# Four-chunk FP32 sums of query-key products by GpSimd additions and accumulating DMAs, gate products ahead of softmax, and four gate buffers

## The chip, the cores and the metric

The kernel runs on one NeuronCore of a Trainium2 chip. The metric is the device time of one execution in microseconds (us), and lower is better. Times vary by some 0.3% between executions, so every comparison below is between kernels run in turn on the same chip. The granted TensorE clock was 1.0.

The profile names engines briefly: PE is TensorE's matrix multiplication, PEld its weight loads, DVE is VectorE, ACT is ScalarE, POOL is GpSimd, SP the queue that issues most DMAs. "L839" is a line of the kernel's source; the line numbers of the two kernels differ.

## The reference, cut to what matters

```python
xn = layernorm(x)                                  # x: 2048 x 640, bf16
# A: sliding, dilated attention, 32 heads of 20, window of 8 keys, 2 apart
q, k, v = split(xn @ wqkv)
logits = einsum("bhsd,bhswd->bhsw", q, k_window) * 20 ** -0.5
o = einsum("bhsw,bhswd->bhsd", softmax(logits), v_window)
# B: bilinear gated feed-forward, 1536 wide
h = (xn @ w_gate) * (xn @ w_up)
return x + o @ wo + h @ w_down
```

The sequence is worked in four blocks of 512 positions. The 640 channels of q and k lie in five chunks of 128 partitions. A logit is a sum over 20 channels that lie in four partitions of each of the five chunks: VectorE multiplies q by shifted k, and TensorE, with a 128x32 matrix of ones and zeros, adds up partitions and chunks.

## The kernel before

A small scheduler in the kernel orders the tasks of five in-order engines by an own model of durations and by priorities (a lower number goes first). It fixes the order when the program is built; on the chip an engine that waits holds everything behind it. The three parts that the change touches follow.

The last block's products are summed over pairs of chunks in FP32 before they reach TensorE:

```python
def pair_add(j, s, n, q0, f, parts):          # f: the two FP32 product tiles, 128 x 1024
    a, b = PRD32[f[0]], PRD32[f[1]]
    o = s[:, q0:q0 + 2, :]                    # bf16
    def go():
        op("pool", lambda e: e.tensor_tensor(o, a[:], b[:], ALU.add), r=[a[:], b[:]], w=[o], ..., occ=2.36, lock=True)
        free.extend(f)
    yield Task("pool", go, r=[a[:], b[:]], w=[o], prio=5, lock=True)
# ... two pair tiles for each of two half-windows, and chunk 4 alone: six tiles, 24 matmuls for the block's logits
```

Gate and up products. Each half of h is five matmuls into a PSUM bank; ScalarE copies the gate half to SBUF, VectorE multiplies it by the up half and so frees that bank:

```python
yield Task("act", ev, r=[PS[:, hold[0], :]], w=[h], prio=7)
yield Task("dve", mul, r=[h, PS[:, hold[1], :]], prio=15)      # softmax tasks on VectorE: prio 10
```

The attention-weighted values: VectorE multiplies (`PV`), GpSimd adds two halves (`SV<-PV`), TensorE sums partitions.

```python
def ht(j, m):                                  # buffers of h: three sets for four blocks
    return HX[m][:] if j % 3 == 2 else HT[:, j % 3, m, :]
```

Of the kernel before, what the change touches and what calls it, by code (L numbers as in the profile page):

```python
# [6 lines left out]
ALU = mybir.AluOpType  # L7

S = 2048
D = 640  # L10
NCH = 5
# [37 lines left out]
class Sched:  # L49
# [5 lines left out]
    def __init__(self, nc):  # L55
        self.nc = nc
        self.ops = []
        self.state = {}
        self.base = {}
        self.clock = {e: nc.alloc_semaphore(f"clk_{e}") for e in ("act", "pe", "dve", "pool")}  # L60
        self.n_dma = 0
        self.t = {"sp": 0.8, "act": 0.8, "pe": 1.26, "dve": 0.9, "pool": 0.8}
        self.t_lock = 0.0
        self.t_data = 0.0
        self.pe_mode = 0
        self.threads = []
        self.banks = {b: 0.0 for b in range(8)}
        self.seq = 0
        self.groups = {}
        self.n_eng = {e: 0 for e in ENGINES}  # L70
# [55 lines left out]
    def op(self, eng, fn, r=(), w=(), dma=False, name="", occ=None, lat=None, lock=False, nbytes=0, mode=0, group=None, extra=0.0):  # L126
# [17 lines left out]
        if dma:  # L144
            self.t[eng] = start + (0.48 if occ is None else occ)
            self.t_data = max(self.t_data, start + 1.2) + nbytes / 280e3
            X.end = self.t_data + 0.8 + extra
        else:
            self.t[eng] = start + occ
            X.end = start + (occ if lat is None else lat)  # L150
# [190 lines left out]
def build_kernel(nc, A_x, A_wqkv, A_wo, B_x, B_w_gate, B_w_up, B_w_down, out):  # L341
# [62 lines left out]
    WIDE = (3,)  # L404
# [6 lines left out]
    STATS = sb("STATS", [128, NT, 16], FP32)  # L411
    MV = sb("MV", [128, NT, 16], FP32)
    SD = sb("SD", [128, NT, 16], FP32)
# [10 lines left out]
    def ht(j, m):  # L424
        return HX[m][:] if j % 3 == 2 else HT[:, j % 3, m, :]

    WPOS = (2, 0, 1)
# [234 lines left out]
    def proj_qk():  # L662
# [11 lines left out]
        for j in (2, 3):  # L674
            yield have("xnt", 4 * j + 3)
            for m in range(NCH):
                for which in (0, 1):
                    if which or j not in WIDE or m == NCH - 1:
# [33 lines left out]
    def slot():  # L712
        return free.pop(0)
# [7 lines left out]
    def products():  # L721
        for j in range(NJ):
            slots = []
            if j in WIDE:
                yield from wide(j, slots)
            for r in (1, 0):
                for c in range(NCH - 1 if j in WIDE else 0, NCH):
                    yield num(4, "qk", 0, j, c)
                    yield num(4, "qk", 1, j, c)
                    yield lambda: len(free) > 0  # L730
                    n = slot()
                    s = PRD[n]
                    kv, rk = k_view(j, r, c, 0, 4)
                    q = QT[:, j, c, :]
                    qb = q.unsqueeze(1).to_broadcast([128, 4, JB])

                    def go(s=s, qb=qb, kv=kv, q=q, rk=rk):
                        op("dve", lambda e: e.tensor_tensor(s[:], qb, kv, ALU.mult), r=[q, rk], w=[s[:]],  # L738
                           name=f"prod{j}_{r}_{c}", occ=1.15, lock=True)

                    yield Task("dve", go, r=[q, rk], w=[s[:]], prio=20 + j, lock=True)
                    slots.append((n, s, r))
            K.spawn(logits(j, slots))

    def q_bank(j, c, hold):
        def go(b):
            mms([(PS[:, b, :], 0, c, j * JB, JB)], b, f"p0_{j * JB}")
            hold.append(b)
            for _ in range(4):
                bump("qk", 0, j, c)  # L750

        yield have("xnt", 4 * j + 3)
        yield Task("pe", go, r=[wcols(0, NCH - 1, c), XNT[:, NCH - 1, j * JB:(j + 1) * JB]], prio=8, banks=1, keep=1)

    def wide(j, slots):
        for c0 in (0, 2):
            hold = {}
            for c in (c0, c0 + 1):
                hold[c] = []
                yield num(4, "qk", 1, j, c)  # L760
                K.spawn(q_bank(j, c, hold[c]))
            last = None
            for r in (1, 0):
                yield lambda: len(free) > 0
                n = slot()
                s = PRD[n]
                parts = []
                for q0 in (0, 2):
                    f = []
                    for c in (c0, c0 + 1):  # L770
                        yield lambda: len(hold[c]) > 0 and len(free) > 0
                        k = slot()
                        f.append(k)
                        o = PRD32[k]
                        kv, rk = k_view(j, r, c, q0, 2)
                        q = PS[:, hold[c][0], :]
                        qb = q.unsqueeze(1).to_broadcast([128, 2, JB])

                        def go(o=o, qb=qb, kv=kv, q=q, rk=rk):
                            X = op("dve", lambda e: e.tensor_tensor(o[:], qb, kv, ALU.mult), r=[q, rk], w=[o[:]],  # L780
                                   name=f"prow{j}_{r}_{c}_{q0}", occ=1.17)
                            if r == 0 and q0 == 2:
                                K.free_bank(hold[c][0], X)

                        yield Task("dve", go, r=[q, rk], w=[o[:]], prio=20 + j)
                    K.spawn(pair_add(j, s, n, q0, f, parts))
                slots.append((n, s, r, parts))

    def pair_add(j, s, n, q0, f, parts):
        a, b = PRD32[f[0]], PRD32[f[1]]  # L790
        o = s[:, q0:q0 + 2, :]

        def go():
            op("pool", lambda e: e.tensor_tensor(o, a[:], b[:], ALU.add), r=[a[:], b[:]], w=[o], name=f"padd{j}_{n}_{q0}",  # L794
               occ=2.36, lock=True)
            free.extend(f)
            parts.append(q0)

        yield Task("pool", go, r=[a[:], b[:]], w=[o], prio=5, lock=True)

    def logits(j, slots):
# [5 lines left out]
        nt = len(slots) // 2  # L807

        def go(*bs):
            for i, e in enumerate(slots):  # L810
                n, s, r = e[:3]
                b, i = bs[1 - r], i % nt
# [30 lines left out]
    def softmax(x):  # L843
# [24 lines left out]
        def attn():  # L868
            op("dve", lambda e: e.tensor_tensor(L[:], L[:], bc(RS[:], 8), ALU.mult), r=[L[:], R], w=[L[:]], name="attn",
# [61 lines left out]
    def unit(u):  # L931
# [33 lines left out]
        def add(x):  # L965
            o, p = SV[u % NS][:, 2 * x:2 * x + 2, :], slots[x]
            X = op("pool", lambda e: e.tensor_tensor(o, p[:, :, 0, :], p[:, :, 1, :], ALU.add), r=[p[:]], w=[o],  # L967
# [8 lines left out]
        def adder(x, slots=slots, u=u, add=add):  # L976
            yield Task("pool", lambda: add(x), r=[slots[x][:]], w=[SV[u % NS][:, 2 * x:2 * x + 2, :]], prio=10, lock=True)
# [16 lines left out]
        if len(pend) == 3 or u == NU - 1:  # L994
# [29 lines left out]

    def gu(j):
# [10 lines left out]
        elif j == 2:  # L1036
            yield have("atx", 1)
        else:
            yield num(8, "dn", j - 3)
        if j:  # L1040
            yield have("gu", j - 1)
        for m in range(NF):
            h = ht(j, m)
            if j == 1 and m == 6:
                yield num(NJ, "lg")
            hold = []
# [9 lines left out]
            def after(h=h, hold=hold, j=j, m=m):  # L1056
# [11 lines left out]
                yield Task("dve", mul, r=[h, PS[:, hold[1], :]], prio=15)  # L1068
# [18 lines left out]
    def dn(j):  # L1087
        yield num(NF, "h", j)
        yield num(NCH, "ot", j)
        if j:  # L1090
            yield num(8, "dn", j - 1)
        for st in range(4):
            t = 4 * j + st
            pieces = ((0, 320), (320, 480), (480, 640)) if t == NT - 1 else ((0, 320), (320, 640))
            for nb, (c0, c1) in enumerate(pieces):
                rows = slice(st * TS, (st + 1) * TS)
                cols = slice(c0, c1)
                wid = c1 - c0
                hold = []
                yield have("xr", t)  # L1100

                def go(b):
                    n = NF + NCH
                    dst = PS[:, b, 0:wid]
                    for i in range(n):
                        if i < NF:
                            l, x = ht(j, i)[:, rows], WD[:, i, cols]
                        else:
                            l, x = OT[:, j, i - NF, rows], WO[:, i - NF, cols]
                        op("pe", (lambda l, x, i: lambda e: e.matmul(dst, l, x, start=(i == 0),  # L1110
                                                                    stop=(i == n - 1)))(l, x, i),
                           r=[l, x], w=[PS[:, b, :]], name=f"dn{t}_{nb}_{i}", occ=wid / 2400 + 0.0025, lat=0.25)
                    hold.append(b)
                    bump("dn", j)

                def fin_thread(t=t, nb=nb, cols=cols, hold=hold, wid=wid):
                    o, xr = FOUT[:, t % 2, cols], XR[:, t % NXR, cols]

                    def fin():
                        b = hold[0]  # L1120
                        X = op("dve", lambda e: e.tensor_tensor(o, PS[:, b, 0:wid], xr, ALU.add), r=[PS[:, b, :], xr], w=[o],  # L1121
                               name=f"fin{t}_{nb}", occ=0.15 + wid / 960)
                        K.free_bank(b, X)

                    def store():
                        if t == NT - 1:
                            f, d = o, ohbm[t * TS:(t + 1) * TS, cols]
                        else:
                            f, d = FOUT[:, t % 2, :], ohbm[t * TS:(t + 1) * TS, :]
# [97 lines left out]
```

## Time and profile before

| | before |
|---|---|
| time, median (3 runs) | 271.63 us (271.47 to 271.93) |
| profiled span | 269.7 us |
| TensorE busy | 264.3 us, 98% |
| VectorE busy | 231.9 us, 86% |
| GpSimd busy | 115.2 us, 43% |

The page of the profile gives busy time of each engine, its share of the span and the number of instructions; its part 4 gives the shares of the chain of work that ended last.

```profile
PE 264.3 (98%) x1791; PEld 152.7 (57%) x1791; DVE 231.9 (86%) x294; ACT 98.4 (36%) x175; POOL 115.2 (43%) x65
...
PE 96%; DVE 2%; DMA 1%; issue 0%; DVEq 0%
```

TensorE bounds the kernel: nearly the whole chain is its own work. A gain has to come from TensorE's work or from its waits. The chain in order of time (start us, length us, what) has one place after the start-up where it leaves TensorE:

```profile
108.68 13.05 PE PS L1052 x60
121.73 0.08 issue
...
122.62 0.69 DVE HT L1061
...
123.36 18.52 PE PS L1052 x85
```

Timeline: start us, us, engine, line, operation, number of instructions, and in brackets the idle time before them.

```profile
121.57 1.24 PE L1052 MATMUL PS<-XNT,WG 128*128 128x512 bf16 x5
123.36 1.25 PE L1052 MATMUL PS<-XNT,WU 128*128 128x512 bf16 x5 [0.55 <-DVE HT L1061]
```

The five matmuls from 121.57 us take 5 x 0.216 = 1.08 us, so the next could have started at 122.65 us and started at 123.36 us: 0.71 us late, of which the profile shows 0.55 us as idle after the last matmul's end. The second group waited for a bank that a gate product on VectorE frees. VectorE's timeline at that time:

```profile
115.22 1.22 DVE L845 TENSOR_TENSOR SM<-LOG 128x1024 f32<-128x1024 bf16 x1
116.47 3.19 DVE L845 TENSOR_TENSOR SM<-SM 128x512 f32<-128x512 f32 x2
...
121.48 1.22 DVE L869 TENSOR_TENSOR LOG<-LOG,RS 128x2048 bf16<-128x2048 bf16 x1
122.62 2.47 DVE L1061 TENSOR_TENSOR HT<-HT,PS 128x512 bf16<-128x512 bf16 x4
```

GpSimd's timeline at that time:

```profile
115.38 3.27 POOL L967 TENSOR_TENSOR SV<-PV 128x1024 bf16<-128x1024 f32 x1 [11.69 <-DVE PV L962]
```

The VectorE lines are the end of the second softmax (sums, reciprocal, scaling) and then four gate products. The two small sums at 116.47 us took 3.19 us together, against 1.15 us for the same two in the first softmax (at 68.05 us), and GpSimd's addition beside them took 3.27 us instead of 2.36.

### The profile page before, as it was taken

Reading aid. Unit: us, or ns where it says so; the run is one execution under the profiler, and the core shown is the slowest. Engines: PE = TensorE matmul, PEld = TensorE weight load, DVE = VectorE, ACT = ScalarE, POOL = GpSimd, SP = SyncE. Lnnn points to the kernel's source line nnn. Section 1 sums busy time; section 2 is a strip of 40 time slices with the busy share of each in tenths; the row PEclk is TensorE's granted clock in tenths of the full one; section 3 lists DMA queues with packets and bytes.
Section 4 is the critical chain, followed back from the end, with each engine's and each line's share of the span. In section 5 each row is a group of like instructions: output and inputs, shape, how many; then the busy total and the mean of one; then the engine's idle time right before and its main releaser. Section 6 shows DMA issues by size and latency. Waiting matters only on the chain.

```text
span 269.7 us, 4474 instructions
## 1 busy us (share of the span) xinstructions
PE 264.3 (98%) x1791; PEld 152.7 (57%) x1791; DVE 231.9 (86%) x294; ACT 98.4 (36%) x175; POOL 115.2 (43%) x65
## 2 busy tenths in 40 slices
PE   7999999999999999999999999999999999999995
PEld 4896965544444444443444446764447767654775
DVE  4778899999999997999999999989999998984221
ACT  2469998557632123632324422015240120033000
POOL 1000000000018763042776676957868679755000
DMA  7966479322325934901295333555333655220101
GB/s 209 366 198 86 99 124 381 158 97 97 104 44 163 216 66 130 282 5 30 52 256 125 86 79 79 155 153 130 79 80 106 175 135 148 66 81 2 49 27 50
DMA packets 39717, 33.49 MB, mean 124 GB/s; under 512 B 15376, under 2 KB 38416, under 8 KB 39696
## 3 DMA queue, kind: packets, MB, share of 16 engines
q1 hardware_dynamic: 39408, 33.15, 45.8%
q8 instruction: 14, 0.23, 0.4%
q10 hardware_dynamic: 288, 0.05, 0.1%
q14 instruction: 7, 0.06, 0.1%
HBM read 25.08 MB, written 5.26 MB: 112 GB/s over the span
## 4 chain that ended last, share of the span: by engine, by line
PE 96%; DVE 2%; DMA 1%; issue 0%; DVEq 0%
PE PS L1052 38%; PE PS L1110 28%; PE PS L610 24%; PE PS L816 3%; PE PS L1008 2%; DMA XST<-in_A_x_dram 1%; PE PS L569 1%; DVE STATS L525 0%; DVE XNT L578 0%; DVE HT L1061 0%; DVE XNS L543 0%; DVE FOUT L1121 0%; DVE MV L528 0%; DVE SD L536 0%; DVEq L319 0%
## 5 line engine op out<-in xcount | busy, mean ns | idle before, releaser
L967 POOL TENSOR_TENSOR SV<-PV 128x1024 bf16<-128x1024 f32 x40 | 94.7, 2378 | 48.4 <-DVE PV L962 48.3
L962 DVE TENSOR_TENSOR PV<-VX,PS 128x1024 f32<-128x1024 bf16 (+1 forms) x56 | 92.7, 1670 | 0.0
L610 PE MATMUL PS<-XNT,WQKV 128*128 128x512 bf16 (+2 forms) x480 | 67.0, 299 | 0.8 <-DVE XNT L578 0.8
L1052 PE MATMUL PS<-XNT,WU 128*128 128x512 bf16 x240 | 59.7, 379 | 0.5 <-DVE HT L1061 0.5
L1052 PE MATMUL PS<-XNT,WG 128*128 128x512 bf16 x240 | 59.7, 379 | 0.0
L610 PEld LDWEIGHTS PS<-XNT,WQKV 128*128 128x128 bf16 x480 | 43.4, 114 | 23.4 <-DVE XNT L578 1.5
L1110 PE MATMUL PS<-WD,HT 128*128 128x320 bf16 (+1 forms) x300 | 43.3, 294 | 0.0
L615 ACT ACTIVATE HT<-PS 128x512 bf16<-128x512 f32 x36 | 21.5, 597 | 53.2 <-PE PS L1052 53.1
L1052 PEld LDWEIGHTS PS<-XNT,WU 128*128 128x128 bf16 x240 | 23.3, 98 | 29.3 <-DVE HT L1061 1.0
L1052 PEld LDWEIGHTS PS<-XNT,WG 128*128 128x128 bf16 x240 | 23.2, 98 | 28.7 <-issue 0.8
L738 DVE TENSOR_TENSOR PRD<-QT,KT 128x2048 bf16<-128x2048 bf16 x32 | 36.8, 1218 | 0.0
L1110 PEld LDWEIGHTS PS<-WD,HT 128*128 128x128 bf16 x300 | 28.5, 98 | 11.6 <-issue 1.3
L794 POOL TENSOR_TENSOR PRD<-PRF,PRF 128x1024 bf16<-128x1024 f32 x8 | 18.8, 2357 | 35.5 <-DVE PRF L780 35.5
L1121 DVE TENSOR_TENSOR FOUT<-PS,XR 128x320 bf16<-128x320 f32 (+1 forms) x33 | 15.8, 478 | 18.3 <-PE PS L1110 18.2
L1061 DVE TENSOR_TENSOR HT<-HT,PS 128x512 bf16<-128x512 bf16 x36 | 24.1, 682 | 6.8 <-PE PS L1052 5.6
L1110 PE MATMUL PS<-WO,OT 128*128 128x320 bf16 (+1 forms) x165 | 27.1, 295 | 0.0
L835 POOL MEMSET LOG<- 32x6 bf16 (+6 forms) x7 | 0.4, 95 | 46.6 <-ACT LOG L827 46.6
L1017 ACT ACTIVATE OT<-PS 128x512 bf16<-128x512 f32 x20 | 10.5, 597 | 25.1 <-PE PS L1008 25.1
L1110 PEld LDWEIGHTS PS<-WO,OT 128*128 128x128 bf16 x165 | 15.9, 98 | 5.9
L780 DVE TENSOR_TENSOR PRF<-PS,KT 128x1024 f32<-128x1024 f32 x16 | 19.0, 1218 | 0.3 <-PE PS L816 0.2
L525 DVE BATCH_NORM_STATS2 STATS<-XST 128x6 f32<-128x320 bf16 x32 | 14.7, 469 | 2.0 <-DMA XST<-in_A_x_dram 2.0
L947 ACT ACTIVATE PS<-ATX 128x512 f32<-128x512 bf16 x8 | 4.8, 598 | 27.4 <-DVE PV L962 27.4
(47 smaller groups left out, 162.3 us busy)
## 6 DMA issues: line engine op xcount, KB each, us to landing
VX<-v_scratch SPq DMA_DIRECT2D x80, 130.0 KB, 2.9
XST<-in_A_x_dram SPq DMA_DIRECT2D x16, 160.0 KB, 6.3
v_scratch<-VST SPq DMA_DIRECT2D x4, 640.0 KB, 4.4
XR<-in_A_x_dram SPq DMA_DIRECT2D x16, 160.0 KB, 3.3
out_dram<-FOUT SPq DMA_DIRECT2D x15, 160.0 KB, 2.0
WG<-in_B_w_gate_dram SPq DMA_DIRECT2D x1, 1920.0 KB, 7.6
WU<-in_B_w_up_dram SPq DMA_DIRECT2D x1, 1920.0 KB, 11.8
WD<-in_B_w_down_dram SPq DMA_DIRECT2D x1, 1920.0 KB, 8.6
```

Of the source, the lines that this page charges most:

```text
L525: op("dve", lambda e: e.bn_stats(o, a), r=[a], w=[("st", t, i)], name=f"bn{t}_{i}", occ=0.49)
L610: op("pe", (lambda o, l, x, c, first: lambda e: e.matmul(o, l, x, start=first, stop=(c == NCH - 1)))(o, l, x, c, first), r=[l, x], w=[o], ...
L615: X = op("act", (lambda o, i: lambda e: e.activation(o, i, ACT.Copy))(o, i), r=[i], w=[o], name=name, occ=0.12 + n * 0.9e-3)
L738: op("dve", lambda e: e.tensor_tensor(s[:], qb, kv, ALU.mult), r=[q, rk], w=[s[:]], name=f"prod{j}_{r}_{c}", occ=1.15, lock=True)
L780: X = op("dve", lambda e: e.tensor_tensor(o[:], qb, kv, ALU.mult), r=[q, rk], w=[o[:]], name=f"prow{j}_{r}_{c}_{q0}", occ=1.17)
L794: op("pool", lambda e: e.tensor_tensor(o, a[:], b[:], ALU.add), r=[a[:], b[:]], w=[o], name=f"padd{j}_{n}_{q0}", occ=2.36, lock=True)
L962: op("dve", lambda e: e.tensor_tensor(p, vw, a, ALU.mult), r=[vv] + rk, w=[p], name=f"pv{u}_{x}_{r0}", occ=0.09 + 1.1 * nr)
L967: X = op("pool", lambda e: e.tensor_tensor(o, p[:, :, 0, :], p[:, :, 1, :], ALU.add), r=[p[:]], w=[o], name=f"pva{u}_{x}", occ=2.36, lock= ...
L1052: op("pe", (lambda l, x, c: lambda e: e.matmul(PS[:, b, :], l, x, start=(c == 0), stop=(c == NCH - 1)))(l, x, c), r=[l, x], w=[PS[:, b, :] ...
L1061: X = op("dve", lambda e: e.tensor_tensor(h, h, PS[:, hold[1], :], ALU.mult), r=[h, PS[:, hold[1], :]], w=[h], name=f"h{m}_{j}", occ=0.65)
L1110: op("pe", (lambda l, x, i: lambda e: e.matmul(dst, l, x, start=(i == 0), stop=(i == n - 1)))(l, x, i), r=[l, x], w=[PS[:, b, :]], name=f" ...
L1121: X = op("dve", lambda e: e.tensor_tensor(o, PS[:, b, 0:wid], xr, ALU.add), r=[PS[:, b, :], xr], w=[o], name=f"fin{t}_{nb}", occ=0.15 + wi ...
```

## The change

The intent: fewer logit matmuls in the last block (four tiles instead of six), by summing four chunks in FP32, partly on GpSimd and partly by DMAs that add into their destination; no gate product behind a softmax; and more freedom of order through a fourth set of h buffers and a down projection in two parts. The diff has some 300 lines; this is its core.

```diff
-    WIDE = (3,)
+    QUAD = {3: (1, 0)}
+    BY_DMA = (((0, 0), (0, 2)), ((1, 0), (1, 2)))
     ...
+    def sum32(j, r, q0, p, a, b):
+        x, y = PRD32[a][:], PRD32[b][:]
+        if (r, q0) in BY_DMA[p]:
+            yield Task("pool", lambda: op("pool", lambda e: e.dma_start(x, y, accum_op=ALU.add), r=[x, y], w=[x], dma=True,
+                                          name=name, occ=0.88, acc=3.3), r=[x, y], w=[x], prio=4)
+        else:
+            yield calm
+            yield Task("pool", lambda: op("pool", lambda e: e.tensor_tensor(x, x, y, ALU.add), r=[x, y] + tokens(), w=[x], ...
+        free.append(b)
     ...
+            if acc:                                    # the scheduler's model of such a DMA
+                self.t_acc = max(self.t_acc, start + 2.8) + acc
     ...
+    def calm():                                        # GpSimd additions stay out of a softmax
+        return all(("sm", x) in done or count.get(("logits", x), 0) < 2 for x in range(2))
     ...
     def ht(j, m):
-        return HX[m][:] if j % 3 == 2 else HT[:, j % 3, m, :]
+        if j == 3:                                     # block 3 uses the dead normalized input of blocks 0 to 2
+            return XNT[:, m % NCH, m // NCH * JB:(m // NCH + 1) * JB]
+        return HX[HXM[m]][:] if j == 2 else HT[:, j, m, :]
     ...
+                if on_pool(j, m):                      # some gate products on GpSimd, after the second softmax
+                    yield Task("act", uev, r=[PS[:, hold[1], :]], w=[us], prio=7)
+                    yield Task("pool", pmul, r=[h, us], w=[h], prio=HP_PRIO, lock=True)
+                    return
-                yield Task("dve", mul, r=[h, PS[:, hold[1], :]], prio=15)
+                yield Task("dve", mul, r=[h, PS[:, hold[1], :]], prio=H_PRIO)      # H_PRIO = 9
     ...
-                yield Task("pe", go, prio=40, banks=1, r=[WD[:], WO[:]])           # 12 down + 5 output matmuls
+        yield Task("pe", down, prio=41, banks=1, keep=..., r=[WD[:], WO[:]])       # 12, and in another task 5
```

GpSimd still makes eight additions of 128x1024 for the sums. The order of instructions shows the last block's logits on TensorE behind 30 gate/up groups of five matmuls, where there were 24 in front of them, and 11 of the 48 gate products on GpSimd.

## The prediction

> **What bounds it now.** TensorE. The page shows PE busy 264.3 of 269.7 us, and the chain of waits that ended last is 96% PE. Along that chain TensorE starts at 5.38 us, is busy without a break from about 16.8 us, waits once, and ends at 267.0 us. Its pieces run at one rate: 80 gate/up matmuls of 512 columns in 17.27 us (216 ns each), 136 down/output matmuls of 320 columns in 18.58 us (137 ns). The one wait, in the chain at 121.73 to 123.36 us, is 1.63 us: a gate/up matmul wants a PSUM bank that a VectorE gate product must free, and the timeline shows VectorE in the second softmax until 122.6 us, four gate products behind it. The granted clock is 1.00 throughout.
>
> **What the change does.**
> 1. Last block's logits: six product tiles become four, so 24 matmuls become 16. The 24 took 1.41 us, the 40 of another block 2.27; I expect 0.95, saving 0.46 us, all on the chain.
> 2. Gate products ahead of softmax on VectorE: the 1.63 us wait should go, all on the chain.
> 3. GpSimd still makes eight 128x1024 additions (2.36 us each), but now in a chain over four chunks, plus four accumulating DMAs of 0.52 MB. The Trainium skill ("DMA: Bandwidth & Descriptors", section on the anatomy of a GpSimd DMA) gives 2.0 us plus bytes over 436 GB/s: 3.2 us for a plain copy; reading the destination as well should make it 4 to 6. No trace here has one. Instruction order puts these logits 6 gate/up units later on TensorE (30 in front instead of 24): 107.3 becomes about 113.7 us. Adding up VectorE products (1.13 us apart), DMAs and additions, the last sum ends near 112 to 113 us: just in time; DMAs one microsecond slower each would cost 1 to 3 us.
> 4. That starts the second softmax about 6 us later. Before, VectorE was 97% busy from 125 to 163 us and 94% to 237; so 11 of the 48 gate products go to GpSimd (estimate 1.2 us each, half a 2.36 us addition; ScalarE copies their up half first, 0.6 us each), which takes 11 x 0.68 = 7.5 us off VectorE. GpSimd's busy sum rises from 115 to about 128 us, VectorE's falls to about 224. By my sums both are over 90% busy from 128 to 245 us, coupled through three product buffers: tight, perhaps a microsecond of waits at the attention sums.
> 5. Separate gate buffers for block 3 and the split down projection remove order constraints where TensorE has no wait now: no gain.
>
> **Prediction.** 271.6 - 0.5 - 1.6 + about 0.4 of new waits = **269.9 us**, 8 in 10 between 268.6 and 272.0. Faster by over 2%: 0.02. Within 2%: 0.94. Slower by over 2%: 0.04.
>
> **What would show it.** Right: PE busy about 263.8; no PE wait on a gate product near 122 us; those 16 matmuls in about 0.95 us near 113 us. Wrong: a PE wait before those logits, released by GpSimd or a DMA (step 3); waits before the attention-sum matmuls (step 4); a gate product on GpSimd well over 1.2 us.
>
> **What would make it wrong.** Accumulating DMAs of 8 us or more each would stall TensorE by over 5 us at the in-order logits. GpSimd additions held off by VectorE instructions with two SBUF inputs (the 3.27 us addition at 115.4 us, during the softmax, against 2.36 elsewhere hints at it) would starve the attention sums.

## The result, and the profile after

| | before | after |
|---|---|---|
| time, median of 6 runs each | 271.6 us (271.3 to 271.93) | 271.5 us (271.33 to 271.63) |
| ratio | | 0.9996, 95% interval 0.9983 to 1.0009 |
| TensorE, VectorE, GpSimd busy | 264.3, 231.9, 115.2 us | 262.3, 223.3, 129.2 us |

The time is within 2%, as forecast, but the forecast gain of 1.7 us did not come: 0.1 us did, which is no difference. The page after:

```profile
PE 262.3 (97%) x1765; PEld 152.2 (56%) x1783; DVE 223.3 (83%) x283; ACT 104.6 (39%) x186; POOL 129.2 (48%) x80
...
PE 86%; DMA 5%; POOL 3%; DVE 2%; issue 2%; ACT 0%; SPq 0%; POOLq 0%; ACTq 0%
...
PRF<-PRF POOLq DMA_DIRECT2D x4, 512.0 KB, 9.4
```

(TensorE's 262.3 us come with 1765 of its 1783 matmul records; some are missing, so this is not to be read as less work.) The chain now runs through DMA and GpSimd for 8% of the span, and the last line, of the DMA issues (number, KB of each, median us from issue to landing), says that an accumulating DMA took 9.4 us to land. The chain in order of time shows where this lies:

```profile
96.98 9.32 DMA PRF<-PRF
...
106.49 2.85 POOL PRD L861 x2
...
111.11 2.35 POOL PRF L843
...
113.53 2.37 POOL PRD L861
...
115.94 0.40 PE PS L883 x4
```

This tells what was followed back, not what TensorE lost. Its timeline does that. Here are the places between the logits of block 2 and those of block 3, the last, at which it started late:

```profile
78.08 2.34 PE L883 MATMUL PS<-PRD,G 128*32 128x512 bf16 x40
...
100.87 1.24 PE L1127 MATMUL PS<-XNT,WG 128*128 128x512 bf16 x5
102.66 1.03 PE L1127 MATMUL PS<-XNT,WU 128*128 128x512 bf16 x4 [0.55 <-DVE HT L1136]
103.53 1.24 PE L1127 MATMUL PS<-XNT,WG 128*128 128x512 bf16 x5
104.96 1.25 PE L1127 MATMUL PS<-XNT,WU 128*128 128x512 bf16 x5 [0.19 <-DVE HT L1136]
...
114.77 0.83 PE L883 MATMUL PS<-PRD,G 128*32 128x512 bf16 x12
115.94 0.40 PE L883 MATMUL PS<-PRD,G 128*32 128x512 bf16 x4 [0.34 <-POOL PRD L861]
116.27 1.25 PE L1127 MATMUL PS<-XNT,WG 128*128 128x512 bf16 x5
```

A group of five has 1.08 us, so the group after 100.87 us was due at 101.95 us (its first record is missing: "x4", so it began one matmul ahead of 102.66 us, at 102.44), and that after 103.53 us at 104.61 us; each waited for a gate product. The last of the four logit tiles waited for GpSimd. And this is why the gate products were late on VectorE:

```profile
95.47 1.22 DVE L817 TENSOR_TENSOR PRF<-PS,KT 128x1024 f32<-128x1024 f32 x1
96.82 0.69 DVE L1136 TENSOR_TENSOR HT<-HT,PS 128x512 bf16<-128x512 bf16 x1
100.56 1.23 DVE L817 TENSOR_TENSOR PRF<-PS,KT 128x1024 f32<-128x1024 f32 x1 [3.05 <-DMA PRF<-PRF]
101.70 0.68 DVE L1136 TENSOR_TENSOR HT<-HT,PS 128x512 bf16<-128x512 bf16 x1
103.08 1.22 DVE L817 TENSOR_TENSOR PRF<-PS,KT 128x1024 f32<-128x1024 f32 x1 [0.70 <-DMA PRF<-PRF]
104.22 1.27 DVE L1136 TENSOR_TENSOR HT<-HT,PS 128x512 bf16<-128x512 bf16 x2
106.33 1.23 DVE L817 TENSOR_TENSOR PRF<-PS,KT 128x1024 f32<-128x1024 f32 x1 [0.84 <-DMA PRF<-PRF]
```

VectorE's products of the second half need tiles that the DMAs still read. Three times VectorE stood still for a DMA, 3.05, 0.70 and 0.84 us, with a gate product behind it in its order. The four DMAs were issued at 88.20, 90.45, 93.53 and 96.98 us and landed 7.2 to 10.1 us later. Each is 128 pieces of 4096 bytes; in the trace's records of the DMA engines the first piece started 2.9 us after the first issue and a piece took 327 ns in the median, so as an estimate 128 pieces on 16 engines, one at a time on each, are 8 x 0.327 = 2.6 us. From the start of the first piece to the end of the last, the four took 14.8 us. With the pieces taken in order, 128 to a DMA, the four ran one after the other, 3.6 to 4.2 us each. So the 9.4 us is not the time of one transfer: the second to the fourth DMA also waited behind the one before, and began 4.2 to 4.7 us after their issue. All the while the DMA engines also moved the value loads, 16 DMAs of 130 KB, issued between 84.73 and 97.78 us.

### One number that the start-up does not blur

The start of a run moves by up to a microsecond between executions (one profiled run below began its first projections 1.1 us late, waiting for the input's statistics). So I compare in the profiles what I call *TensorE's stretch*: from the first logit matmul of block 2 to the start of the last VectorE addition before the final store. It holds all that the change touches except the tail, and TensorE's work in it differs only by the eight matmuls.

| kernel | from | to | stretch | against before |
|---|---|---|---|---|
| before | 77.84 | 267.03 | 189.19 us | |
| after | 78.08 | 267.50 | 189.42 us | +0.23 |

The ends that are not shown yet, in TensorE's timeline before (its logits of blocks 2 and 3 and the group after them):

```profile
77.84 2.34 PE L816 MATMUL PS<-PRD,G 128*32 128x512 bf16 x40
...
107.20 1.48 PE L816 MATMUL PS<-PRD,G 128*32 128x512 bf16 x24
108.61 1.25 PE L1052 MATMUL PS<-XNT,WG 128*128 128x512 bf16 x5
```

VectorE's last addition before:

```profile
267.03 0.33 DVE L1121 TENSOR_TENSOR FOUT<-PS,XR 128x160 bf16<-128x160 f32 x1 [0.85 <-PE PS L1110]
```

And after:

```profile
267.50 0.33 DVE L1222 TENSOR_TENSOR FOUT<-PS,XR 128x160 bf16<-128x160 f32 x1 [0.85 <-PE PS L1209]
```

Split for these two kernels: from the logits of block 2 to those of block 3 there were 29.36 us before and 36.69 after, with 30 more matmuls of 216 ns (6.47 us), so **0.86 us lost** in late starts behind gate products. From the first logit matmul of block 3 to the next gate/up group, 1.41 us (107.20 to 108.61, 24 matmuls) became 1.50 us (114.77 to 116.27, 16 matmuls). The softmax wait of 0.71 us went.

### The profile page after: what moved, and what is told of

Read it like the earlier page. It is cut to its first block, busy times and chain, and to the rows that moved or that the text cites. A ratio compares the mean times of both kernels' runs of the same rounds, so it can differ in the third digit from the quotient of the medians. Undisturbed runs are those within 1.5% of the kernel's fastest.

```text
span 269.8 us, 4454 instructions
## 1 busy us (share of the span) xinstructions
PE 262.3 (97%) x1765; PEld 152.2 (56%) x1783; DVE 223.3 (83%) x283; ACT 104.6 (39%) x186; POOL 129.2 (48%) x80
## 4 chain that ended last, share of the span: by engine, by line
PE 86%; DMA 5%; POOL 3%; DVE 2%; issue 2%; ACT 0%; SPq 0%; POOLq 0%; ACTq 0%
PE PS L1127 29%; PE PS L1209 28%; PE PS L622 24%; DMA PRF<-PRF 3%; PE PS L883 3%; POOL PRD L861 2%; PE PS L1076 2%; DMA WQKV<-in_A_wqkv_dram 2%; DVE PRF L817 1%; POOL PRF L843 1%; DVE HT L1136 1%; PE PS L581 0%; SPq L462 0%; ACT KT L627 0%; DVE XNT L590 0%
## 5 line engine op out<-in xcount | busy, mean ns | idle before, releaser
L1034 POOL TENSOR_TENSOR SV<-PV 128x1024 bf16<-128x1024 f32 x40 | 93.4, 2359 | 24.4 <-DVE LOG L936 16.0
L1127 PE MATMUL PS<-XNT,WU 128*128 128x512 bf16 x233 | 58.1, 379 | 1.0 <-DVE HT L1136 0.7
L1127 PE MATMUL PS<-XNT,WG 128*128 128x512 bf16 x234 | 58.7, 379 | 0.4
L1209 PE MATMUL PS<-WD,HT 128*128 128x320 bf16 x192 | 28.7, 299 | 0.1
L627 ACT ACTIVATE HT<-PS 128x512 bf16<-128x512 f32 x24 | 14.3, 596 | 34.9 <-PE PS L1127 34.8
L843 POOL TENSOR_TENSOR PRF<-PRF,PRF 128x1024 f32<-128x1024 f32 x4 | 9.4, 2347 | 36.6 <-DVE PRF L817 36.6
L1209 PEld LDWEIGHTS PS<-WD,HT 128*128 128x128 bf16 x192 | 18.6, 98 | 8.2 <-issue 0.4
L1136 DVE TENSOR_TENSOR HT<-HT,PS 128x512 bf16<-128x512 bf16 x23 | 15.5, 680 | 5.3 <-PE PS L1127 3.5
L1209 PE MATMUL PS<-WD,XNT 128*128 128x320 bf16 (+1 forms) x108 | 14.5, 284 | 0.0
```

Source lines behind the costliest of these rows:

```text
L627: X = op("act", (lambda o, i: lambda e: e.activation(o, i, ACT.Copy))(o, i), r=[i], w=[o], name=name, occ=0.12 + n * 0.9e-3)
L843: yield Task("pool", lambda: op("pool", lambda e: e.tensor_tensor(x, x, y, ALU.add), r=[x, y] + tokens(), w=[x], name=name, occ=2.36, lock ...
L1034: X = op("pool", lambda e: e.tensor_tensor(o, p[:, :, 0, :], p[:, :, 1, :], ALU.add), r=[p[:]] + tokens(), w=[o], name=f"pva{u}_{x}", occ= ...
L1127: op("pe", (lambda l, x, c: lambda e: e.matmul(PS[:, b, :], l, x, start=(c == 0), stop=(c == NCH - 1)))(l, x, c), r=[l, x], w=[PS[:, b, :] ...
L1136: X = op("dve", lambda e: e.tensor_tensor(h, h, PS[:, hold[1], :], ALU.mult), r=[h, PS[:, hold[1], :]], w=[h], name=f"h{m}_{j}", occ=0.65)
L1209: op("pe", (lambda l, x, i: lambda e: e.matmul(dst, l, x, start=(i == 0), stop=(i == n - 1)))(l, x, i), r=[l, x], w=[PS[:, b, :]], name=f" ...
```

## The experiments

The theory after reading the two traces (**theory A** in the expectations): the change can win 0.71 us at the softmax and about 0.45 us of logit matmuls, and gives both back because accumulating DMAs land late, which holds VectorE's products, the gate products behind them, and GpSimd's last sums. The rivals are named in each expectation. Ten kernels ran, all correct, each five rounds or more against the kernel before on the same chip.

| kernel | median | before, same rounds | ratio, 95% interval | stretch against before |
|---|---|---|---|---|
| e1 before, gates first | 270.89 | 271.38 | 0.9976 (0.9964 to 0.9989) | 188.48, -0.71 |
| e2 after, gates late | 271.53 | 271.38 | 1.0004 (0.9992 to 1.0017) | 189.30, +0.11 |
| e3 after, value loads behind the DMAs | 270.11 | 271.38 | 0.9947 (0.9935 to 0.9960) | 188.04, -1.15 |
| e4 after, scheduler told longer DMAs | 269.94 | 271.38 | 0.9950 (0.9937 to 0.9964) | 188.03, -1.16 |
| e5 after, no DMA sums | 269.81 | 271.46 | 0.9938 (0.9926 to 0.9951) | 188.04, -1.15 |
| e7 after, e3 and e4 together | 270.12 | 271.46 | 0.9947 (0.9935 to 0.9960) | 188.05, -1.14 |
| e8 after, sums in pairs | 270.90 | 271.71 | 0.9980 (0.9954 to 1.0006) | 188.47, -0.72 |
| e9 before, additions off the softmax | 270.85 | 271.46 | 0.9971 (0.9958 to 0.9985) | 188.47, -0.72 |
| e10 e5 with gates late | 270.26 | 271.71 | 0.9951 (0.9936 to 0.9967) | 188.04, -1.15 |
| e11 e5 with no gate products on GpSimd | 273.04 | 271.71 | 1.0051 (1.0036 to 1.0067) | 190.59, +1.40 |

The stretches fall on three steps: 0.71 or 0.72 us below before where the softmax wait is gone, 1.14 to 1.16 below where the eight matmuls are saved too, and above it where something is given back.

### e1: gate products first, in the kernel before

```diff
-                yield Task("dve", mul, r=[h, PS[:, hold[1], :]], prio=15)
+                yield Task("dve", mul, r=[h, PS[:, hold[1], :]], prio=9)
```

> The kernel before, with one number changed: the gate products' priority on VectorE from 15 to 9, so that they go ahead of the softmax. TensorE's instruction order is unchanged. Theory A (my second reading: TensorE's true idle time at 122 us was 0.55 us, its next matmul 0.71 us late, because the 1.63 us piece of the chain ran under matmuls that were still going): that wait goes and nothing else, 271.6 becomes 270.9 us, ratio 0.9974. Theory P (the prediction on record: 1.63 us lost): 270.0 us, ratio 0.994.

Ratio 0.9976, stretch -0.71 us, and no wait for a gate product is left in the list of TensorE's waits. TensorE's order is unchanged, so this measures the softmax wait by itself: it was 0.71 us, not 1.63. Theory P is out: its 0.994 lies below the interval.

The meeting of a softmax sum with a GpSimd addition, the hint above, is still there in e1, the other way round. VectorE's timeline:

```profile
115.67 3.26 DVE L845 TENSOR_TENSOR SM<-LOG 128x1024 f32<-128x1024 bf16 x1 [0.25 <-ACT LOG L860]
```

GpSimd's addition began first here, at 115.51 us, and took its usual 2.35 us, and the sum behind it took 3.26 us instead of 1.22. So the softmax was lengthened by 2 us in e1 too, and the priority alone still removed TensorE's wait.

### e2: the changed kernel with gates late

```diff
-    H_PRIO = 9
-    FIN_PRIO = 8
+    H_PRIO = 15
+    FIN_PRIO = 14
```

> The changed kernel with gate products and final additions back at their old priorities (15 and 14). Theory A: a TensorE wait of 0.5 to 0.7 us on a gate product comes back in the second softmax, 271.5 becomes 272.1 us, ratio to before 1.002. Rival N (the priority is worth nothing in this kernel, since GpSimd takes gate products): 271.5 us, ratio 1.000, no such wait.

My own expectation missed: ratio 1.0004, and no wait came back in the softmax, though the gate products stood behind it again. TensorE's only wait for a gate product in this kernel shows 1.08 us of idle time, where VectorE stands for the DMAs (the group was due 1.08 us after 102.88, at 103.96 us, so it was 1.25 us late):

```profile
105.21 1.25 PE L1127 MATMUL PS<-XNT,WU 128*128 128x512 bf16 x5 [1.08 <-DVE HT L1136]
```

So in the changed kernel the priority is not needed to keep the softmax wait away. Something else in the change does that too; e9 tests a candidate. The edit is not pure, though: with it the scheduler gave GpSimd 12 gate products instead of 11 and changed TensorE's order.

### e3: value loads behind the accumulating DMAs

The order of instructions is the same on every engine; only one wait is added, so the DMAs have the DMA engines to themselves.

```diff
-            ... e.dma_start(x, y, accum_op=ALU.add), r=[x, y], w=[x], dma=True,
+            ... e.dma_start(x, y, accum_op=ALU.add), r=[x, y], w=[x, ("acc", r, q0)], dma=True,
-                rk = [("vscr", "pad")] + [...]
+                rk = [("acc", r, q0) for p in BY_DMA for r, q0 in p] + [("vscr", "pad")] + [...]
```

> The changed kernel, same instruction order on every engine, but the value loads wait for the four accumulating DMAs, which so have the DMA engines alone. Theory A (part of the 7.2 to 10.1 us to landing is a shared queue with the 2.1 MB of value loads from 84.7 to 97.8 us): landings fall to 6 to 7 us, VectorE's 4.6 us of waits for these DMAs to under 1 us, TensorE's late starts between 100 and 116 us from about 1.35 to under 0.4 us, time 270.5 us, ratio 0.996. Rival B (an accumulating DMA takes this long by itself): landings stay over 9 us in the median, time 271.5, ratio 1.000. Rival C (VectorE's and GpSimd's waits are beside the point, the loss sits elsewhere): landings fall, time stays 271.5.

The tile view of the FP32 products, with the DMAs' line (durations of the issue on GpSimd, in ns), who waited for them (us, times) and the times to landing:

```profile
L839 POOL DMA_DIRECT2D PRF<-PRF x4: 862/866/1009, 87.8 to 96.6; - x4
...
  DVE PRF L817: 0.2, 1
...
DMA to landing us min/median/max: 4.7/5.3/6.3
```

TensorE's timeline at the last block's logits in the same kernel:

```profile
113.55 1.05 PE L883 MATMUL PS<-PRD,G 128*32 128x512 bf16 x16
114.53 1.25 PE L1127 MATMUL PS<-XNT,WG 128*128 128x512 bf16 x5
```

Landings fell from 7.2/9.4/10.1 us (shortest, median, longest) to 4.7/5.3/6.3 (I had expected 6 to 7), VectorE's waits for them from 4.6 to 0.2 us, and TensorE's waits for gate products to none. The 16 logit matmuls took 0.98 us (113.55 to 114.53), and the last sum no longer came late. Ratio 0.9947, stretch -1.15 us. Rival B (the DMA takes that long by itself) and rival C (the loss sits elsewhere) are out. Both kernels have the same work in the same order, so 189.42 - 188.04 = 1.38 us is what the late landings cost TensorE: 0.86 us through gate products (the stretch between the two blocks' logits is 35.83 us here, 36.69 there) and 0.52 us at the logits (0.98 against 1.50 us).

### e4: the scheduler told the longer landing

```diff
-                self.t_acc = max(self.t_acc, start + 2.8) + acc
+                self.t_acc = max(self.t_acc, start + 3.9) + acc
-                                          name=name, occ=0.88, acc=3.3), ...
+                                          name=name, occ=0.88, acc=3.7), ...
```

> The changed kernel, its scheduler told that an accumulating DMA lands 7.6 us after issue and each next 3.7 us later (6.1 and 3.3 before). It then puts a gate product ahead of the product that waits for a buffer, and the last block's logits one gate/up pair later on TensorE. Theory A (in-order VectorE holding a gate product behind a buffer that a DMA still reads is what TensorE waits for): late starts between 100 and 118 us fall from 1.35 to under 0.5 us, DMA landings stay 7 to 10 us, time 270.5 us, ratio 0.996. Rival C: 271.5 us, ratio 1.000.

Landings stayed at 7.7/9.1/9.6 us, and still the loss is gone: ratio 0.9950, stretch -1.16 us. One more gate product now stands ahead of a product that waits, and the logits stand one gate/up pair later. VectorE still waited for DMAs, 1.9 us in all, but with nothing behind it that TensorE needed at the time. GpSimd also took 12 gate products here instead of 11, so e4 does not say which of the moves counted; but it shows that the loss can go while the landings stay long. It is not the landing itself that costs, it is what an in-order engine holds behind it; the kernel's cost model, too short by 1.1 us at the first landing (7.2 us against 6.1), made that order.

### e5: all twelve additions on GpSimd

```diff
-    BY_DMA = (((0, 0), (0, 2)), ((1, 0), (1, 2)))
+    BY_DMA = ((), ())
```

> The changed kernel with all twelve additions on GpSimd and no accumulating DMA. Theory A (the DMAs' late landings held VectorE's products and so the gate products): VectorE has no wait for a DMA; GpSimd needs 12 x 2.36 = 28.3 us for the sums instead of 18.9, from about 81.6 us, so the last sum ends at about 112 to 116 us and the logits wait 0 to 2 us for it; TensorE waits for gate products under 0.5 us; 270.3 to 271.3 us, ratio 0.996 to 0.999. Rival C (the DMAs are beside the point): 271.5, ratio 1.000.

This was better than I expected, ratio 0.9938 and 269.81 us, and the last sum came earlier than with the DMAs. GpSimd's timeline of it:

```profile
81.16 2.35 POOL L843 TENSOR_TENSOR PRF<-PRF,PRF 128x1024 f32<-128x1024 f32 x1 [32.05 <-DVE PRF L817]
...
87.47 6.98 POOL L843 TENSOR_TENSOR PRF<-PRF,PRF 128x1024 f32<-128x1024 f32 x3 [1.10 <-DVE PRF L817]
94.53 2.35 POOL L861 TENSOR_TENSOR PRD<-PRF,PRF 128x1024 bf16<-128x1024 f32 x1
...
106.21 4.78 POOL L861 TENSOR_TENSOR PRD<-PRF,PRF 128x1024 bf16<-128x1024 f32 x2
```

Twelve additions fill GpSimd almost without a gap from 81.16 to 110.99 us. In the changed kernel, with eight, the last ended at 115.89 us (113.53 plus 2.36): GpSimd stood idle for DMA-fed VectorE products in between. The four DMAs, meant to relieve GpSimd, made the result about 4.4 us later (4.9 us by the clock, of which 0.5 is a later start, 81.64 against 81.16 us). Kernels of different calls are not compared to 0.1%, so e5 and e4 (269.81 and 269.94 us) are equal as far as this shows; their stretches are.

### e7: both mends

> The changed kernel with both mends: value loads behind the accumulating DMAs, and the scheduler told the longer landing. Theory A (both remove the same TensorE waits, so they do not add): 270.0 us, ratio 0.995, as either alone. Rival: they add, 269.0 us or less.

The edit is that of e3 and that of e4 together. Ratio 0.9947, stretch -1.14 us: they do not add, so they remove the same waits.

### e6 and e8: the change without its four-chunk sum

The old pair sums put back into the changed kernel, everything else as changed. The core of the edit:

```diff
-                yield from wide(j, rows[j], holds[j])
+                yield from pairs(j, rows[j])              # the old wide() and pair_add()
-    ORDER = ((0, "n"), (1, "n"), (2, "n"), (3, "n"), (3, "w"))
+    ORDER = ((0, "n"), (1, "n"), (2, "n"), (3, "w"), (3, "n"))
```

> The changed kernel with the last block's products summed in pairs as before (six tiles, 24 matmuls, no accumulating DMA), everything else as changed: gates first, gate buffers, gate products on GpSimd, split down projection, GpSimd additions out of the softmax. Theory A (outside the four-chunk sum the change is worth the one 0.7 us wait): no TensorE wait on a gate product, 270.9 us, ratio 0.9975. Rival R (the rest of the change is what cancels the gain): 271.5 us or more.

This one was refused before it ran: a weighted-value product could overwrite the softmax reciprocal before VectorE had read it, since the kernel leaves out waits between near VectorE instructions (and the kernel sent had block 3's order as changed). With that allowance cut from four instructions to three and the order as above, it ran as e8:

> The refused kernel mended (one more wait between near VectorE instructions): the changed kernel with the last block's products summed in pairs as before (six tiles, 24 matmuls, no accumulating DMA), everything else as changed. Theory A (outside the four-chunk sum the change is worth the one 0.7 us wait): no TensorE wait on a gate product, logits of 1.41 us, 270.9 us, ratio 0.9975. Rival R (the rest of the change is what cancels the gain): 271.5 us or more, ratio 1.000.

Ratio 0.9980 with a wide interval (0.9954 to 1.0006); the time alone does not decide. Its profiled run fell on a late start. The stretch, which leaves the start out, is 188.47 us, -0.72, with no TensorE wait on a gate product. So outside the four-chunk sum the change is worth the softmax wait and nothing more, and rival R is out by the profile.

### e9: GpSimd's additions kept out of the softmax, in the kernel before

```diff
+    def calm():
+        return all(("sm", x) in done or count.get(("logits", x), 0) < 2 for x in range(2))
     ...
+            yield calm
             yield Task("pool", lambda: add(x), r=[slots[x][:]], ...
```

(with a token that makes the wait hold on the chip, as in the change)

> The kernel before, same order on every engine; the only edit holds GpSimd's value additions until the second softmax has ended (one addition, at 115.4 us, is moved). Theory D (TensorE's wait at 122 us came from a collision: the two softmax sums that take 1.15 us in the first softmax took 3.19 us beside a GpSimd addition that took 3.27 instead of 2.36): the two sums take 1.15 us, the wait of 0.55 us goes, 270.9 us, ratio 0.9975, though gate products still stand behind the softmax. Rival G (the order of gate products alone made it): wait stays, 271.5 us, ratio 1.000.

VectorE's timeline in the second softmax of this kernel:

```profile
115.52 1.22 DVE L851 TENSOR_TENSOR SM<-LOG 128x1024 f32<-128x1024 bf16 x1
116.78 1.15 DVE L851 TENSOR_TENSOR SM<-SM 128x512 f32<-128x512 f32 x2
...
120.89 2.47 DVE L1068 TENSOR_TENSOR HT<-HT,PS 128x512 bf16<-128x512 bf16 x4
```

GpSimd's first addition there:

```profile
121.06 2.35 POOL L973 TENSOR_TENSOR SV<-PV 128x1024 bf16<-128x1024 f32 x1 [17.06 <-DVE LOG L875]
```

The two sums take 1.15 us instead of 3.19, the addition 2.35 instead of 3.27, the gate products start at 120.89 us instead of 122.62, although still behind the softmax, and the wait is gone: ratio 0.9971, stretch -0.72. The times fit an exclusive hold: before, the addition's record begins at 115.38 us, one VectorE sum ran to 116.44, the addition ended 2.21 us after that, at 118.65 (it usually takes 2.36; its record reads 3.27), and the two small sums ended 1.01 us later, at 119.66 (they usually take 1.15). So these times fit to within some 0.15 us. In e1, where the addition began first, it was the VectorE sum that took 2 us longer. The Trainium skill describes this ("SBUF — State Buffer", section "Who interferes with whom"): a VectorE instruction with two SBUF inputs contends with a GpSimd instruction that reads SBUF, and one blocks the other entirely. These two traces agree. So in the kernel before, TensorE's 0.71 us had two sufficient cures, the priority (e1) and this guard against additions in the softmax (e9). The change carries both, which would explain why taking one away in e2 brought nothing back. No run lifts the guard in the changed kernel, where GpSimd's gate products also relieve VectorE (rival N of e2), so what keeps the wait away there is not shown.

### e10: the variant without DMAs, gates late

The edit is that of e2 on e5.

> The all-GpSimd variant (no accumulating DMA) with gate products and final additions back at their old priorities, behind the softmax. Theory D (what made TensorE wait in the softmax was the collision with a GpSimd addition, and the changed kernel keeps those additions out): no wait comes back, 269.9 us, ratio 0.994, as with gates first. Rival P2 (gate priority is worth its 0.7 us by itself): 270.5 us, ratio 0.9965.

The stretch is 188.04 us, the same as e5's, with no wait on a gate product; the ratio, 0.9951 (0.9936 to 0.9967), includes theory D's 0.994 and also P2's 0.9965, just. The profile decides against P2: with the guard in place, and 13 gate products on GpSimd (11 in e5; this edit changes the order too), the priority is worth nothing.

### e11: the variant without DMAs, all gate products on VectorE

```diff
-    HP_MAX = 2
+    HP_MAX = 0
```

> The all-GpSimd variant with all 48 gate products on VectorE, none on GpSimd. Theory S (step 4 of the prediction: VectorE was near its limit from 125 us on and needed the 7.5 us of relief): TensorE waits of 1 us or more at the attention sums, 271 us or more, ratio 0.998 or higher. Rival T (there is slack; a later order of the sums costs TensorE nothing): 269.9 us, ratio 0.994, no such wait.

Slower than before: ratio 1.0051, and the stretch is 190.59 us, 2.55 more than e5's. TensorE waits at an attention sum:

```profile
232.28 0.82 PE L1076 MATMUL PS<-SV,SEL 128*32 128x512 bf16 x10
234.51 0.39 PE L1076 MATMUL PS<-SV,SEL 128*32 128x512 bf16 x2 [1.40 <-POOL SV L1034]
```

The two late matmuls were due at 232.28 + 10 x 0.063 = 232.91 us (12 such take 0.76 us in the chain at the other sums) and came at 234.51: 1.6 us, released by GpSimd, which in turn had waited for VectorE. Most of the rest lies at the next sums, where output matmuls wait for ScalarE's copies (0.18 us of idle twice at 255 us). So theory S holds: once the logits come 6 us later, VectorE does need the relief that gate products on GpSimd give it. The order of TensorE's instructions changes with this edit, so the 2.55 us are the price of the whole reordering, not of the waits alone.

## Why the prediction was right or wrong, point by point

- **TensorE bounds the kernel, time within 2%: right.** The profile after and every experiment agree; the time, 271.5 us, lay inside the range (268.6 to 272.0). The centre, 269.9 us, was 1.6 us off and the gain that it stated did not appear.
- **Step 2, "the 1.63 us wait should go, all on the chain": the wait went, its size was wrong.** I took a piece of the chain's length for idle time of TensorE. It measured 0.71 us by TensorE's timeline and by e1 (-0.71). The cause that I named, gate products behind the softmax, was not the whole of it; the softmax itself was 2 us longer than it had to be through the collision with a GpSimd addition (e9). 0.92 us of forecast gain never existed.
- **Step 1, "saving 0.46 us, all on the chain": right in work, given back.** The 16 matmuls take 0.98 us when they do not wait (e3), against 1.41 for 24: 0.43 us. In the change they took 1.50, since the last tile came late.
- **Step 3, the accumulating DMAs, "4 to 6" us each, "just in time": this is where the gain went.** The Trainium skill's fit for a GpSimd DMA ("DMA: Bandwidth & Descriptors", section on the anatomy of a GpSimd DMA: 2.0 us plus bytes over 436 GB/s) gives 3.2 us for a copy of 0.52 MB; no run here has such a copy. My estimate for the accumulating kind, made from that, was about right when it runs alone (4.7 to 6.3 us, e3) and wrong beside the value loads (7.2 to 10.1 us). The same page says ("Queues, rings and completion order") that a DMA engine takes turns between the queues that have work for it; the two queues' pieces are mixed in this trace, and taking one away shortened the other. The busy times by stretch of the kernel before had shown me the DMA engines 61% busy from 80.2 to 107.3 us, and I did not put the new DMAs beside that. I also looked for the wait at the logits only. It came in two places: 0.86 us through gate products held behind VectorE's blocked products, and 0.52 us at the logits. The warning, over 5 us of stall at the logits with DMAs of 8 us or more each, was wrong as well: the median landing was 9.4 us and the stall there 0.52. The last sum, forecast near 112 to 113 us, ended at 115.89.
- **Step 4, "perhaps a microsecond of waits at the attention sums": none came in the change.** The relief on GpSimd was needed and enough (e11 without it: +2.55 us). GpSimd's gate product took 1.15 to 1.16 us, as estimated at 1.2.
- **Step 5, no gain from buffers and the split: consistent.** e8, which has both, gains no more than e1, which has neither. That they cost nothing is not shown separately.

The sum, as forecast: -0.46 - 1.63 + about 0.4. As measured in the stretch: -0.43 - 0.71 + 1.38 = +0.24, against +0.23 read directly. The step that failed is the third term, new waits, 0.4 against 1.38 us, and with it the second, 1.63 against 0.71.

The lowest median here is that of the change without its DMAs (e5): 269.81 us, 0.6% under the kernel before. e3, e4, e7 and e10 have the same stretch to 0.02 us, so none of the five is shown to be the best.

## What to carry to other kernels

Before counting a wait as gain, measure it on the waiting engine's own timeline, from the start due to the start seen; a piece of the chain of waits overlaps with work still in flight. When a change puts a transfer between in-order engines, cost it beside whatever else uses the DMA engines at that time, and ask what stands behind the instruction that will wait for it: here 0.86 of the 1.38 us lost came through gate products that had nothing to do with the transfer. And when two guards can each remove a wait, test them apart, since taking out either shows nothing.

## What the Trainium skill lacked or had wrong

- "DMA: Bandwidth & Descriptors" gives no time for an accumulating DMA. Here one of 0.52 MB within SBUF, with the DMA engines to itself, landed after 4.7 to 6.3 us, against 3.2 us by the page's fit for a copy, which no run here has; its pieces of 4096 bytes took 341 ns each in the median (327 in the changed kernel), which is 192 GB/s over 16 engines (200), one piece at a time on each, and issuing one kept GpSimd busy for 0.86 to 1.01 us. Beside 2.1 MB of other loads it was 7.2 to 10.1 us, the wait behind the DMA before it included.
- "TensorE: Matmul & The Clock Gate", section "Back-to-back issue gap", gives about 131 ns for sustained matmuls of 512 columns in a stream of weight load and matmul pairs, and calls N / 2.4 + 2.5 ns an isolated figure. Here such streams run at 216 ns each without a break (80 in 17.27 us), which is the second figure.
- "SBUF — State Buffer" names the shared read interface of VectorE and GpSimd rightly, but no page gives the size of it in a mixed kernel: one 2.36 us addition, begun in a softmax, lengthened it by 2 us (3.19 against 1.15 us; in e1, where the addition began first, 3.26 against 1.22) and cost TensorE 0.71 us before.
